# 46 instead of 36 filler products ahead of a TensorE-bound kernel, and 20 more behind the last turn of batch 0's q

## The chip, the core and the metric

The kernel runs on one core of a Trainium2 chip. The metric is the device time of one execution in microseconds (us); lower is better. The engines of the core are TensorE (PE in the profile, its weight loads PEld), VectorE (DVE), ScalarE (ACT), GpSimd (POOL) and SyncE (SP, which only starts transfers here). Each engine works through its own list of instructions in order, and waits where an instruction needs a result of another engine or of a transfer.

## The reference

Eight batches, each with 8 heads, 576 tokens and a head size of 64. Attention without softmax, each row normalised by its root mean square, then a gated linear unit with a causal convolution over 5 tokens as gate:

```python
kv = np.einsum('bhsd,bhse->bhde', k, v)
out = np.einsum('bhsd,bhde->bhse', q, kv)
rms = np.sqrt(np.mean(out * out, axis=-1, keepdims=True) + 1e-06)
attn = out / rms * g_norm                       # then (B,H,S,D) -> x of (B, S, 512)
for j in range(5):
    gate_pre += conv_w[j][None, None, :] * xp[:, j:j + S, :]   # xp: x with 4 rows of zeros ahead
gate = 1.0 / (1.0 + np.exp(-gate_pre))
y = (gate * (x @ w_val)) @ w_out                # all float32; the weights arrive as float64
```

## The kernel before

The whole program is one list of 1,235 named steps, PLAN, written out by hand. A step issues a handful of instructions, on one engine in most cases, and the order of the steps is the order of each engine's instructions. No scheduler moves anything afterwards; only the waits are put in automatically, from which tile is read and written by whom. So an engine that waits holds back all that stands behind it in its own list.

What a batch goes through: `load_q`, `load_half` bring q, k, v in; `kv_product` (L440) makes k^T v on TensorE, in two halves of the heads, into two accumulators; `turn_q_rows` (L477, batches 0 and 1 only) turns q with 24 + 8 + 4 products against an identity, `sort_q` (L484, ACT) copies the turned q out; `kv_copy` (L450, ACT) copies k^T v out; `raw_whole` (L512) multiplies q by it; `square` (L531, ACT), `sums` (L544, DVE), `powers` (L552, POOL) and `normalise` (L561, DVE) normalise the rows; `turn_x` and `keep_x` turn them; then gate, value product and output product follow. PSUM is one pool of eight banks, and every product step takes the next free one.

In front, the plan lets TensorE begin before any data are there. `start_warm n` (L430) issues n products of the identity's first 32 columns with themselves, into a bank that nobody reads:

```python
def start_warm(n):
    for _ in range(n):
        nc.tensor.matmul(warm_bank()[0:TB, 0, 0:TB], ident[:, 0:TB], ident[:, 0:TB], start=True, stop=True)
```

A float32 product shows in the trace as two records. TensorE's list in front is: 36 fillers; `turn_q_rows 0 3`, `0 2`, `0 0` (24 products, wait for q of batch 0); `kv_product 0 0` (waits for the first halves of k and v); `turn_q_rows 0 1` and `0 4` (12 products); `turn_cw` (L414, one small transpose of the convolution's weights, cw); `kv_product 0 1` (waits for the second halves of k and v); `raw_whole 0 3`, `0 4`, `0 2`, `0 0`, `0 1`; then `turn_q_rows` of batch 1.

`turn_cw` waits for cw in float32, which a chain of steps `narrow_weight cw 0 n` makes from the 64-bit input on ACT and DVE. On ACT the list is: `narrow_weight cw 0 1` and `0 2`, `warm_up` (a table load), `sort_q 0 0`, `sort_q 0 1`, `narrow_weight cw 0 3` (L372), `sort_q 0 4`, `0 3`, `kv_copy 0 0`, `0 1`, `sort_q 0 2`, then steps on the first weight block (wval) and the squares of batch 0. So cw's third step stands behind a copy of `turn_q_rows 0 1`'s result. DVE makes its last two steps of cw (L375, L389) behind that, and only behind `keep_cw` (L418 to L420) begins with wval (L380, L363, L385).

SP's list of loads is in order too: `load_q_rows 1 1` overwrites the place of batch 0's q, so it waits until `turn_q_rows 0 4` has read it, and all later loads stand behind it.

Of the kernel before, what the change touches and what calls it, by code (L numbers as in the profile page):

```python
# [18 lines left out]
PLAN = """  # L19
load_q_rows 0 1; stage_weight cw 0; load_q_rows 0 0; load_half v 0 0; load_half k 0 0; narrow_weight cw 0 5;  # L20
narrow_weight cw 0 6; narrow_weight cw 0 0; load_half v 0 1; load_half k 0 1; narrow_weight cw 0 1;
narrow_weight cw 0 2; warm_up; stage_weight wval 1; stage_weight wval 0; start_warm 36; turn_q_rows 0 3;
turn_q_rows 0 2; turn_q_rows 0 0; kv_product 0 0; turn_q_rows 0 1; sort_q 0 0; sort_q 0 1; narrow_weight cw 0 3;
narrow_weight cw 0 4; narrow_weight cw 0 7; turn_q_rows 0 4; turn_cw; keep_cw; kv_product 0 1; sort_q 0 4;
sort_q 0 3; kv_copy 0 0; kv_copy 0 1; narrow_weight wval 1 5; narrow_weight wval 1 0; sort_q 0 2; raw_whole 0 3;
load_q_rows 1 1; narrow_weight wval 1 1; narrow_weight wval 1 6; narrow_weight wval 1 2; raw_whole 0 4;
raw_whole 0 2; load_q_rows 1 0; narrow_weight wval 0 0; narrow_weight wval 0 5; square 0 3; stage_weight wval 3;
# [821 lines left out]
```

## Time and profile before

| what | before |
|---|---|
| median of 3 runs | 306.25 us (304.12 to 307.25) |
| profiled execution, first to last instruction (span) | 304.6 us |
| PE busy | 294.8 us (97%) |
| PEld busy | 232.4 us (76%) |
| DVE busy | 269.2 us (88%) |
| ACT busy | 193.7 us (64%) |
| POOL busy | 114.9 us (38%) |
| mean granted TensorE clock | 0.993 |

The span is the profiled execution's own time from its first to its last instruction; the medians are of executions without a profile and hold what lies around the span as well. The page does not show that part by itself. Busy times are of instructions, so an engine that waits is not busy. The granted clock is a share of TensorE's full clock, from events that the trace records; ahead of the first event the trace has no record of it, and the page then prints full speed.

The chain of the page goes back from the last instruction, at each step to what released it. A stage row (a stretch of time, asked for by its bounds) gives for each engine the busy time and the number of instructions in that stretch, then the granted clock, the busy share of the DMA engines and GB/s.

### The profile page before, as it was taken

To read this page: it belongs to the slowest core of one execution; us is meant where nothing else is said; L and a number is where in the kernel's file an instruction comes from. 1 tells how busy PE (TensorE), PEld (TensorE's weight loads), DVE (VectorE), ACT (ScalarE), POOL (GpSimd) and SP (SyncE) were. 2 spreads that over 40 slices of the span, in tenths; PEclk is the share of its full clock that TensorE was granted. 3 is DMA by queue.
4 is the path that set the end of the run, shared out by engine and by line. 5 is a ranking of instruction groups with operands and counts; after the bars stand their busy time and mean duration, and the time that the engine had idled before them with its cause. 6 is when DMAs were issued, how large, how long until landed. Compare 5 with 4: busy or idle time off the path is not lost.

```text
span 304.6 us, 8977 instructions
## 1 busy us (share of the span) xinstructions
PE 294.8 (97%) x3441; PEld 232.4 (76%) x3441; DVE 269.2 (88%) x474; ACT 193.7 (64%) x596; POOL 114.9 (38%) x127
## 2 busy tenths in 40 slices
PE   7899999999999999999999999999999999999993
PEld 7788778877787785777778757787878588888582
DVE  1169999999999999999999999999999999999612
ACT  1569989999768664884586547683787354535220
POOL 3027354406568217364338352345536631000000
PEclk9979999999999999999999999999999999999999
DMA  7999998088569756988689477927411621112423
GB/s 269 343 368 343 272 302 210 4 230 269 154 147 329 231 163 167 269 220 260 173 253 294 111 175 232 326 72 214 114 48 30 169 80 34 36 42 64 103 69 103
DMA packets 32074, 55.53 MB, mean 182 GB/s; under 512 B 6166, under 2 KB 14358, under 8 KB 32032
## 3 DMA queue, kind: packets, MB, share of 16 engines
q1 hardware_dynamic: 29520, 49.76, 55.7%
q0 software_dynamic: 1632, 3.17, 4.1%
q10 hardware_dynamic: 880, 2.03, 1.8%
q8 instruction: 27, 0.44, 0.6%
q14 instruction: 15, 0.12, 0.1%
HBM read 39.21 MB, written 9.44 MB: 160 GB/s over the span
## 4 chain that ended last, share of the span: by engine, by line
PE 89%; DVE 5%; DMA 2%; issue 1%; ACT 1%; DVEq 0%; ACTq 0%; SPq 0%
PE a L774 18%; PE cb L774 14%; PE va L682 13%; PE val L633 11%; PE vc L682 6%; PE kvps L440 6%; PE raw L501 5%; PE out L720 5%; PE vb L682 4%; PE qTps L477 4%; PE raw L512 2%; PE xTps L583 2%; DMA qs<-in_q_dram 2%; DVE gate L621 2%; DVE xs L667 1%
## 5 line engine op out<-in xcount | busy, mean ns | idle before, releaser
L552 POOL TENSOR_TENSOR rt<-ss,mhalf 128x8 f32<-128x8 f32 (+3 forms) x38 | 68.9, 1822 | 101.0 <-DVE ss L544 100.8
L621 DVE SCALAR_TENSOR_TENSOR gate<-xT,cwT,gate 128x576 f32<-128x576 f32 x128 | 101.8, 809 | 1.0
L571 ACT ACTIVATE x<-raw,rt 128x64 f32<-128x64 f32 x252 | 55.8, 351 | 7.2 <-POOL rt L552 4.2
L604 POOL DMA_DIRECT2D xT<-y x48 | 26.4, 557 | 25.5 <-DVE ot L784 14.0
L633 PE MATMUL val<-xT,wval 128*128 128x288 f32 x128 | 33.0, 411 | 0.0
L774 PE MATMUL a<-wsum,sums 128*128 128x256 f32 x128 | 32.4, 382 | 0.0
L628 ACT ACTIVATE gate<-gate 128x576 f32<-128x576 f32 x32 | 22.0, 692 | 11.7 <-DVE gate L621 11.4
L633 PEld LDWEIGHTS val<-xT,wval 128*128 128x128 f32 x128 | 23.5, 190 | 6.5 <-ACT xT L590 0.4
L544 DVE TENSOR_REDUCE ss<-sq 128x8 f32<-128x520 f32 (+1 forms) x40 | 24.7, 627 | 2.9 <-ACT sq L531 2.5
L774 PEld LDWEIGHTS a<-wsum,sums 128*128 128x128 f32 x128 | 24.0, 190 | 4.1 <-issue 0.6
L535 ACT ACTIVATE sq<-raw 128x256 f32<-128x256 f32 (+1 forms) x70 | 22.4, 403 | 7.3 <-PE raw L501 7.1
L682 PE MATMUL va<-xs,vsum 128*128 128x288 f32 x96 | 26.6, 409 | 0.0
L615 ACT ACTIVATE gate<-xT,cwT 128x576 f32<-128x576 f32 x32 | 25.2, 811 | 1.5 <-DVE gv L646 1.3
L646 DVE TENSOR_TENSOR gv<-gv,gate 128x576 f32<-128x576 f32 x32 | 23.6, 750 | 0.9 <-ACT gate L628 0.8
L682 PEld LDWEIGHTS va<-xs,vsum 128*128 128x128 f32 x96 | 18.0, 190 | 5.1 <-ACT x L571 0.4
L611 POOL COPY xT<-xT 128x124 f32<-128x124 f32 x32 | 17.5, 585 | 10.5 <-ACT xT L590 10.5
L501 PEld LDWEIGHTS raw<-kv,qT 64*64 64x64 f32 x1008 | 16.4, 134 | 5.3 <-issue 3.0
L440 PEld LDWEIGHTS kvps<-v,k 64*64 64x64 f32 x1008 | 15.9, 135 | 3.7 <-issue 1.9
L501 PE MATMUL raw<-kv,qT 64*64 64x64 f32 x1008 | 18.7, 221 | 0.0
L440 PE MATMUL kvps<-v,k 64*64 64x64 f32 x1008 | 17.6, 220 | 0.0
L774 PE MATMUL cb<-wsum,sums 128*128 128x256 f32 x64 | 16.9, 386 | 0.1
L774 PE MATMUL cb<-wout,gv 128*128 128x256 f32 x64 | 16.8, 385 | 0.0
(111 smaller groups left out, 542.3 us busy)
## 6 DMA issues: line engine op xcount, KB each, us to landing
qs<-in_q_dram SPq DMA_DIRECT2D x96, 140.0 KB, 4.2
out_dram<-ot SPq DMA_DIRECT2D x140, 64.0 KB, 1.7
k<-in_k_dram SPq DMA_DIRECT2D x14, 576.0 KB, 6.3
v<-in_v_dram SPq DMA_DIRECT2D x12, 576.0 KB, 6.5
xT<-y SPq DMA_DIRECT2D x48, 64.0 KB, 2.7
xT<-y POOLq DMA_DIRECT2D x48, 64.0 KB, 3.3
y<-in_moe_w_val_dram SPq DMA_DIRECT2D x4, 512.0 KB, 11.4
w_wout<-in_moe_w_out_dram SPq DMA_DIRECT2D x4, 512.0 KB, 6.3
```

What stands on the lines that cost most here:

```text
L440: nc.tensor.matmul(st["kvps", b][s][r * D:(r + 1) * D, i], st["k", b, i][rows, r, cols], st["v", b, i][rows, r, cols], start=(j == 0), sto ...
L501: nc.tensor.matmul(st["raw", b, c][r][cols, to * D:(to + 1) * D], st["qT", b][rows, hp, first:first + D], kvs[b % 2][rows, hp, :], start=T ...
L544: nc.vector.reduce_sum(out=st["ss", b][:, FIRST[c]:FIRST[c] + n], in_=st["sq", b, c][:, 0:n], axis=AX.X)
L552: nc.gpsimd.tensor_tensor(out=st["rt", b][:, which], in0=st["ss", b][:, which], in1=mhalf[:, which], op=ALU.pow)
L571: nc.scalar.activation(out=x[:, to * D:(to + 1) * D], in_=raw[:, h * D:(h + 1) * D], func=AF.Copy, scale=root[:, to:to + 1])
L604: (nc.sync if i % 2 else nc.gpsimd).dma_start(out=xTs[b % 2][i * TB:(i + 1) * TB, :, first:first + P], in_=y[a * TB:(a + 1) * TB, i])
L615: nc.scalar.activation(out=gate[:], in_=xTs[b % 2][:, jt, HALO:SX], func=AF.Copy, scale=cwT[:, K - 1, jt:jt + 1])
L621: nc.vector.scalar_tensor_tensor(out=gate[:], in0=xTs[b % 2][:, jt, tap * TB:tap * TB + S], scalar=cwT[:, tap, jt:jt + 1], in1=gate[:], op ...
L633: nc.tensor.matmul(val[:], wval[:, kc, jt * P:(jt + 1) * P], xTs[b % 2][:, kc, HALO + n * SV:HALO + (n + 1) * SV], start=(kc == 0), stop=( ...
L646: nc.vector.tensor_tensor(out=both, in0=both, in1=st["gate", b, jt][:], op=ALU.mult)
L682: nc.tensor.matmul(st[bank, "val", b, mj][:], weights_[:, k], tokens()[:, k], start=(n in (0, 1, 3) and k == 0), stop=(k == NK // 2 - 1), ...
L774: nc.tensor.matmul(st[bank, i, p], tokens()[:, k], weights_[:, k], start=(n < 2 and k == 0), stop=(k == NK // 2 - 1), skip_group_check=True)
```

## The change

`start_warm 36` becomes `start_warm 46`, and a step `start_warm 20` is put between `turn_q_rows 0 4` and `turn_cw`. Nothing else is edited.

```diff
 narrow_weight cw 0 2; warm_up; stage_weight wval 1; stage_weight wval 0;
-start_warm 36; turn_q_rows 0 3;
+start_warm 46; turn_q_rows 0 3;
 turn_q_rows 0 2; turn_q_rows 0 0; kv_product 0 0; turn_q_rows 0 1; sort_q 0 0; sort_q 0 1; narrow_weight cw 0 3;
-narrow_weight cw 0 4; narrow_weight cw 0 7; turn_q_rows 0 4; turn_cw; keep_cw; kv_product 0 1; sort_q 0 4;
+narrow_weight cw 0 4; narrow_weight cw 0 7; turn_q_rows 0 4; start_warm 20; turn_cw; keep_cw; kv_product 0 1; sort_q 0 4;
```

(The first line of the plan is broken in two here, to show its edit alone.) The fillers' bank is now in use until the second batch of them. With that, the banks of three later steps come from other tiles: `turn_cw` takes a bank that ACT has emptied where it took one that TensorE had written alone; `raw_whole 0 2` no longer has a wait on TensorE's own earlier writing, and `raw_whole 0 0` has one. The lists of DVE, ACT, POOL and SP, and all waits in them, stay as they are.

## The prediction

> **What bounds the kernel now.** I read the chain of waits first, for the first 40 us (start, length, what; both in us):
>
> ```profile
> 0.75 5.33 DMA qs<-in_q_dram
> ...
> 6.12 5.05 PE qTps L477 x48
> 11.17 1.21 PE kvps L440 x72
> 12.38 1.49 PE qTps L477 x24
> 13.86 1.19 issue
> 15.05 0.21 PE cwps L414
> ...
> 17.15 6.32 PE raw L512 x40
> 23.47 2.77 PE qTps L477 x48
> ```
>
> Two things stand out. TensorE has nothing to do for 1.19 us ahead of `turn_cw`. And equal work has unequal prices: 48 records of `turn_q_rows` cost 5.05 us at 6.12 and 2.77 at 23.47. So I asked for the groups of TensorE between 6.1 and 10.4, and between 10.6 and 13.9 (busy us, mean ns of one behind the first bar):
>
> ```profile
> L477 PE MATMUL qTps<-ident,qs 128*64 128x128 f32 x39 | 4.5, 424 | 0.7 <-DMA qs<-in_q_dram 0.7
> ...
> L477 PE MATMUL qTps<-ident,qs 128*64 128x128 f32 x35 | 2.5, 287 | 0.0
> ```
>
> The first stretch runs at about half clock, although the stage rows print 1.00 there (no record yet). Next the stages around the drop that is recorded, and a long one behind it:
>
> ```profile
> 13.93:17.34 3.41, 1.73 (x74) 1.59 (x75) 2.53 (x9) 1.86 (x7) 0.00 (x0) 1.00 0.77 253
> 17.34:20.75 3.41, 3.41 (x18) 2.65 (x18) 1.81 (x4) 3.32 (x7) 0.00 (x0) 0.50 1.01 374
> 20.75:23.47 2.72, 2.72 (x26) 2.60 (x27) 1.82 (x5) 1.72 (x4) 2.08 (x2) 1.00 1.04 396
> 22.35:107.90 85.55, 85.55 (x1369) 69.03 (x1367) 84.69 (x147) 73.41 (x225) 41.94 (x37) 1.00 0.76 227
> ```
>
> The clock was 0.50 for 3.41 us. Counted back from 17.34 in steps of 3.41, marks fall at 13.93, 10.51, 7.10 and 3.69; 10.51 is where the turns become fast. So I take it that the clock is set at such marks, by how busy TensorE was since the mark before. The records bear out: 7.10 to 10.51 busy throughout, then full; 3.69 to 7.10 with the hole between fillers and q, no rise; 13.93 to 17.34 busy for 1.73 of 3.41 us, then half.
>
> The last row says what a gain in front is worth later: from 22.35 to 107.90 PE is busy for all 85.55 us, DVE for 84.69. Both are full. The list of DVE's waits from 22.4 to 200 has three lines, 1.3 us in all, the first of them ending at that stretch's start:
>
> ```profile
> DVE ss L544 <- ACT sq L531: 0.9, 1, 0.9
> DVE x L561 <- POOL rt L552: 0.2, 1, 0.2
> DVE gv L646 <- ACT gate L628: 0.2, 1, 0.2
> ```
>
> So a gain reaches the end only as far as DVE gets it too.
>
> **The change, part by part.** *Ten more fillers.* 72 records start at 1.36; the last ends 4.05 us later and one lasts 241 ns (its group), so starts are (4.05 - 0.24) / 71 = 53.7 ns apart, 107 ns a product. 92 records let q's turns begin at 1.36 + 92 x 0.0537 = 6.30 instead of 6.12: **+0.18 us** at once. The hole between 5.41 and 6.12 is gone, the window 3.69 to 7.10 is full, and I expect full clock from 7.10. The half-clock turns cost 4.28 us for 39 records, less the start-up 0.21 us a product; at full clock (2.84 - 0.28) / 47 records give 0.109. So 24 products take 0.80 us to 7.10 (3.8 of them) and 20.2 x 0.109 = 2.20 behind it: 9.30 instead of 11.10. There the next wait is late: the first half of v is issued at 1.20 and lands 8.3 us later, 9.5. `kv_product 0 0` starts at 9.5, **1.6 us earlier**.
>
> *Down to `turn_cw`.* What follows keeps its lengths: `sort_q 0 1` came 2.35 us behind that start (13.45), now 11.85; ACT is busy with `sort_q 0 0` until 11.96, so 11.95, and the chain to `turn_cw` (13.45 to 15.05, 1.6 us) ends at 13.55, 1.5 us earlier. Next late is the second half of v: issued 1.69, landing 12.1 us later, 13.8. `kv_product 0 1` starts at about 13.9 instead of 15.19: **-1.3 us** for it, for `kv_copy` (16.56 to 15.27) and for `raw_whole 0 3` (17.15 to 15.85).
>
> *Twenty more fillers.* No row shows a filler at full clock. Upper end 107 ns a product, 2.14 us for 20; lower end half of that, 1.07, since the turns' price halved (0.21 to 0.109) and `kv_product`'s records follow each other in 1.21 / 72 = 17 ns, so issue sets no floor at 53. I take 1.07. `turn_q_rows 0 4` is issued by 12.0, the fillers end near 13.1, `turn_cw` comes at 13.55: hidden. At 2.14 they would hold `turn_cw` to 14.15 and cost 0.4. The new wait of `turn_cw` on ACT is for a copy ahead of cw's own third step in ACT's list, so it is met: 0.
>
> *The clock drop.* Without filler, the mark at 17.34 saw 51% busy. In the changed kernel 13.93 to 17.34 lacks only some 0.7 us ahead of `raw_whole`, about 80% busy: I expect no drop. `raw_whole`'s 20 products then cost 0.21 us each (half of the 17.34 to 20.75 pace, where about 8 took 3.41), 4.3 us, with 0.4 of waiting for the second `kv_copy`: from 15.85 to 20.55 instead of 23.47, **-2.9 us on TensorE**.
>
> *What ACT and DVE get of it.* ACT goes without a break from `kv_copy` to `narrow_weight wval 1 3` (20.02 to 20.73), so -1.3 there: 19.43. Then it waited 0.99 us for `raw_whole 0 2`, which is now there by 19.1: `square 0 2` at 19.43 instead of 21.72, -2.3. DVE's 0.9 us wait for that square goes; behind it `normalise 0 3` waits for POOL's power (2.06 us behind a sum that ends at 19.55): 21.7, and DVE's list reaches it at 21.8 instead of 23.95: **-2.15 us**. From there DVE has no idle time to give up. TensorE runs up to 2.9 early until it meets DVE's or ACT's results; the chain does at 89 to 108, where it goes over DVE and ACT.
>
> The loads do not spoil this. SP's queue is released by `turn_q_rows 0 4` at 12.2 instead of 13.88, and the DMA engines, at 147 GB/s between 13.86 and 15.05, fill that hole; q of batch 1 landed by 19.2 and is used from 20.55.
>
> **Sum:** +0.18 is inside the -1.3, -1.3 and the drop make -2.9 on TensorE, and DVE lets -2.15 through. The profiled span of 304.6 becomes 302.45; the median 306.25 becomes **304.1 us**. Median and span are 1.65 apart, of which I know no split; a run at 304.12 lies below the profiled span, so executions differ by more than my gain.
>
> The Trainium skill, "TensorE: Matmul & The Clock Gate", Part 1, has the clock at half until a busy window of 3.4 us and windows that run free of the kernel's start; the trace agrees on the length (3.41). It has the clock fall only after about such a window of idleness, and here 1.73 us of 3.41 were busy: the measurement decides (by that rule the second fillers save nothing, rival 2). The phase of the windows, which no single trace shows, makes both gains vary by run. By the same Part an undecoded product costs about 62 ns of sequencer time; the fillers' 53.7 ns are below that, and by 62 the twenty would take 2.5 us, the sum 0.35 less than at 2.14.
>
> **Rivals.**
> 1. *More comes through.* DVE's results may be used later than they are made, so TensorE's -2.9 reaches the end: 303.35. And the unprofiled runs may hold a second window at half clock (3.41 us, 1.7 of loss) that the fillers avoid: down to 301.65. For: the spread of 3.1 us between runs. Against: DVE without idle time. 0.25.
> 2. *One gain alone.* The drop comes anyway, or seldom came: -1.3, 304.95. For: other phases of the marks split the 1.19 us hole. Against: this trace's drop stands right behind it. 0.15.
> 3. *Small products count little as activity.* 32 of 128 columns are used. Then no mark moves: +0.18, 306.4. For: the window 3.69 to 7.10, four fifths busy, did not raise the clock. 0.10.
> 4. *Slower.* As 3, and the second fillers are paced by issue, not by the clock: 2.14 us from 13.85 end at 16.0, so `turn_cw` waits 0.95 us longer. It decides from 1.38 us for the twenty (turns issued by 13.67, cw there at 15.05), 69 ns a product. +1.15: 307.4. Against: `kv_product`'s 17 ns. 0.08.
>
> **How the numbers follow.** The forecast's chance is 0.42, its own range 303.4 to 304.9. The range 301.65 to 306.9 takes in rivals 1 to 3 and leaves out most of 4 and scatter. A measurement tells about 1% from no change: below 303.2 is faster, above 309.3 slower. Faster: most of rival 1 (0.20) and a quarter of the forecast (0.10), 0.30. Slower: a run-to-run shift on top of rival 4, 0.05. Same: the rest.
>
> **What would show it.** The turns at 287 rather than 424 ns from about 7; `turn_cw` near 13.55; the fillers of the second batch 27 ns apart; no 0.50 behind 17; `raw_whole` done near 20.6; DVE early by 2.1 us at 24. Wrong if the clock rises no earlier, if the drop comes back, or if DVE's list shows new waits later on.

## The result, and the profile after

| | before | changed |
|---|---|---|
| median of 18 runs each | 304.5 us | 307.85 us |
| lowest to highest | 304.12 to 307.25 | 305.7 to 311.72 |
| profiled execution, span | 304.6 us | 307.3 us |
| mean granted clock of it | 0.993 | 0.996 |

The changed kernel is slower by a factor of 1.0093, 95% interval 1.0067 to 1.0118; this factor leaves out the run at 311.72 us, which fell in a slower state of the chip. Forecast was 304.1 us, within 301.65 to 306.9. The profile of the changed kernel is of an execution at 309.12 us, above its median; a second one, at 307.07 us, comes below. In the profiled executions the clock is better and the time is worse.

The chain of waits of the changed kernel in front (start, length, what; us):

```profile
1.19 9.62 DMA v<-in_v_dram
10.81 0.04 issue
10.86 1.28 PE kvps L440 x72
12.13 1.46 PE qTps L477 x24
13.60 1.38 PE warm L430 x40
14.98 0.17 PE cwps L414
15.14 1.28 PE kvps L440 x72
```

The hole of 1.19 us ahead of `turn_cw` is gone, and the first turns of q are quick (timeline):

```profile
6.00 3.01 PE L477 MATMUL qTps<-ident,qs 128*64 128x128 f32 x48 [0.39 <-DMA qs<-in_q_dram]
```

These 48 records took 5.05 us in the profile of before. But the chain now begins with v's first half, 9.62 us from issue to landing where the prediction reckoned 8.3. `kv_product 0 1` starts at 15.14; before, it was 15.19. Nothing of the 1.3 us has arrived.

The stages that answer to those shown of before (busy us and count for PE, PEld, DVE, ACT, POOL; then clock, DMA share, GB/s):

```profile
13.93:17.34 3.41, 2.77 (x109) 2.50 (x105) 2.65 (x10) 1.77 (x7) 0.00 (x0) 1.00 0.86 272
17.34:20.75 3.41, 3.34 (x31) 2.92 (x30) 1.85 (x5) 3.35 (x7) 0.00 (x0) 1.00 1.03 373
...
22.35:107.90 85.55, 84.62 (x1347) 67.69 (x1344) 83.81 (x145) 72.33 (x223) 41.40 (x37) 1.00 0.76 225
```

Second row: 1.00 where it was 0.50, so the drop has gone. Last row: PE, busy for all 85.55 us before, lacks 0.93. The waits of TensorE between 17 and 295 us name where (engine, line, releaser: us in total, times, longest):

```profile
PE raw L501 <- issue: 2.1, 2, 1.4
PE kvps L440 <- DMA k<-in_k_dram: 1.2, 1, 1.2
```

In the profile of before neither line is there; its longest wait in that stretch is 0.6 us. And DVE's list from 22.4 to 200 has three new lines of about a microsecond, its first three (the one line of 0.9 us of before, for L531, is gone):

```profile
DVE ss L544 <- ACT sq L535: 1.0, 1, 1.0
DVE qT L463 <- DMA qs<-in_q_dram: 0.9, 1, 0.9
DVE ot L784 <- ACT gv L703: 0.8, 1, 0.8
DVE x L561 <- POOL rt L552: 0.2, 1, 0.2
```

"issue" means that the engine waited for nothing that the profile shows. The chain of the changed kernel at the first of these two places, in the midst of one step's products:

```profile
86.06 1.66 PE raw L501 x100
87.73 0.65 issue
88.38 0.70 PE raw L501 x25
```

and the same step in the profile of before, in one piece:

```profile
87.07 2.10 PE raw L501 x128
```

TensorE stops between two products of one step, with all their operands there. So four questions: why v lands late; why TensorE stops; whether the clock's gain is worth what was reckoned; and what the profile of before stood for.

### The profile page after: what moved, and what is told of

The parts are those of the page before. It is cut to its first block, busy times and chain, and to the rows that moved or that the text cites. A ratio compares the mean times of both kernels' runs of the same rounds, so it can differ in the third digit from the quotient of the medians.

```text
span 307.3 us, 9096 instructions
## 1 busy us (share of the span) xinstructions
PE 293.8 (96%) x3501; PEld 231.1 (75%) x3501; DVE 269.5 (88%) x474; ACT 193.7 (63%) x596; POOL 114.9 (37%) x127
## 3 DMA queue, kind: packets, MB, share of 16 engines
HBM read 39.21 MB, written 9.44 MB: 158 GB/s over the span
## 4 chain that ended last, share of the span: by engine, by line
PE 69%; DMA 13%; DVE 7%; SPq 4%; issue 2%; ACT 2%; POOL 1%; ACTq 0%; DVEq 0%
PE a L774 14%; PE va L682 11%; PE val L633 11%; PE cb L774 10%; PE kvps L440 5%; PE vc L682 5%; PE raw L501 5%; DMA out_dram<-ot 4%; PE vb L682 3%; SPq L806 3%; DMA v<-in_v_dram 3%; DMA qs<-in_q_dram 3%; DMA k<-in_k_dram 2%; PE out L720 2%; DVE gate L621 2%
## 5 line engine op out<-in xcount | busy, mean ns | idle before, releaser
L501 PEld LDWEIGHTS raw<-kv,qT 64*64 64x64 f32 x1008 | 16.9, 134 | 7.6 <-issue 5.4
L501 PE MATMUL raw<-kv,qT 64*64 64x64 f32 x1008 | 19.4, 221 | 2.1 <-issue 2.1
L463 DVE STREAM_TRANSPOSE qT<-qs 128x512 f32<-128x512 f32 x24 | 16.7, 695 | 0.9 <-DMA qs<-in_q_dram 0.9
L774 PE MATMUL cb<-wout,sums 128*128 128x256 f32 x64 | 16.7, 383 | 0.3 <-ACT ot L788 0.3
```

The source lines that it names most:

```text
L501: nc.tensor.matmul(st["raw", b, c][r][cols, to * D:(to + 1) * D], st["qT", b][rows, hp, first:first + D], kvs[b % 2][rows, hp, :], start=T ...
L774: nc.tensor.matmul(st[bank, i, p], tokens()[:, k], weights_[:, k], start=(n < 2 and k == 0), stop=(k == NK // 2 - 1), skip_group_check=True)
```

## The theory, and its rival

One queue in section 3 of the profile's page answers to the added products, first before, then changed:

```profile
q8 instruction: 27, 0.44, 0.6%
```

```profile
q8 instruction: 28, 0.46, 0.6%
```

TensorE's own instructions come during the run, 16 KB at a time (0.44 MB in 27). A float32 product is two weight loads and two products in the trace, 4 instructions; 3,441 PE and as many PEld records make 6,882, and with the semaphore instructions some 7,000, so one transfer is about 256 instructions. I counted TensorE's records (products, weight loads and semaphore instructions) from the start of the trace: every stop inside a step lies at a number of 193 plus a multiple of 256 (3009 and 3521 in the changed kernel). These numbers I call edges. Each of the twelve profiles has as many edges as transfers, 27 or 28. The transfers' times are in the trace's records of the queue.

*Block theory.* 30 more products are 120 instructions, so the edges behind them fall on other steps. That costs (a) a wait where two edges come so close together that the transfer begun at the first isn't there at the second, and (b) in front, where the loads keep all 16 DMA engines busy, a part of v or k that stands behind the 16 KB on its DMA engine. *Rival:* the number of instructions doesn't matter; fillers cost by their time, by the banks that they move, by the power that they draw, or because an earlier schedule makes later loads collide (the rival that the expectations below name).

The Trainium skill, "Runtime: NRT & Kernel Launch", section "Instruction fetch mechanics", describes these transfers: blocks of 16 KiB, 256 instructions, which an engine's sequencer fetches over a DMA queue of its own while it works on the block before. The trace agrees (16 KB, period 256). The Trainium skill calls the crossing of a boundary there "mostly hidden"; it gives TensorE room for 2,048 instructions, and a few lines further on for only two blocks. The waits below come at the very next edge, which fits two blocks and not 2,048; so here the measurement decides.

## The experiments

In the diffs `start_warm n w m` issues n fillers with w columns and m rows of weights, both 32 where not given. Only products that nobody reads are changed; all else is computed as before. Times are medians, with the kernel before on the same chip beside them.

**Each part alone (experiments 1 and 2).**

```diff
-start_warm 36; turn_q_rows 0 3;
+start_warm 46; turn_q_rows 0 3;
```

> Only the first half of the change: 46 fillers in front, none behind the last turn. Block theory: TensorE's instructions (a weight load and a product for each record, so four for each float32 product) arrive in blocks of 256 by 16 KB transfers; ten products more shift all later block edges by 40 instructions. The edge in the turns of q is reached near 6.2 us instead of 8.5, its transfer starts near 8 and holds one part of the first half of v until about 10.8, so the front gains nothing although the turns run at full clock; the clock drop at 17 remains. With 40 the edges fall outside the dense products of batch 3 and 4 (88 and 108 us), so none of the waits of 0.9 and 1.6 us seen there in the changed kernel: 304 to 305 us. Rival theory, that TensorE being earlier makes later loads collide: the same front as before, so also about 304.5, and this run does not tell them apart but prices the half. If ten fillers alone cost the 2 to 3 us, both theories fall.

Measured: 305.46 us (304.26 to 307.16) against 304.8, ratio 1.0022 (0.9997 to 1.0048).

```diff
-turn_q_rows 0 4; turn_cw;
+turn_q_rows 0 4; start_warm 20; turn_cw;
```

> Only the second half: 36 fillers in front, 20 behind the last turn. No drop to half clock at 17 us, raw_whole ends about 1.5 us earlier and DVE is about 1 us early from 24 us on, as in the changed kernel. Block theory: 80 instructions of shift put one pair of block edges 3.0 us apart at batch 3 (near 88 us), none at 108: a wait of 0 to 0.9 us there and the rest of the gain kept, 303.3 to 304.5 us. Rival theory (an earlier schedule makes later loads collide): DVE's 1 us lead is lost and more with it, 306 to 308 us, with the waits at 108 and 142 us there as well.

Measured: 305.55 us (304.83 to 308.25) against 304.8, ratio 1.0022 (0.9995 to 1.0050). Neither part alone is a gain, and neither makes the loss. Both came out above what was expected, and in the first the transfer began at 8.81 us, not near 8, so v was on time in its profile (table below). With 40 more instructions no step of TensorE stops behind 17 us; with 80, one does, near 87 us (the same list of waits as above):

```profile
PE raw L501 <- issue: 0.3, 1, 0.3
```

**Time and count apart (3 and 4).** First the fillers' time without their count: 36 products in all, some of them with 128 columns.

```diff
-start_warm 36; turn_q_rows 0 3;
+start_warm 20 128; start_warm 6; turn_q_rows 0 3;
-turn_q_rows 0 4; turn_cw;
+turn_q_rows 0 4; start_warm 10 128; turn_cw;
```

> The change's filler times with the number of fillers of before: in front 20 products of 128 columns and 6 of 32 (about 4.9 us at half clock, as 46 of 32), behind the last turn 10 of 128 columns (about 1.1 us at full clock, as 20 of 32). 36 in all, so every block edge behind turn_cw is where it was before. Block theory: no waits at 88 and 108 us, the first fetch starts later than 9.5 us, so v lands near 9.5 and turn_cw comes near 13.6 us: the gain that was forecast for the change comes through, 302 to 303 us. Rival theory (the earlier schedule makes later loads collide): as slow as the changed kernel or slower, 306.5 to 309 us, since the schedule is earlier still.

Measured: 306.9 us (306.5 to 307.12) against 304.8, ratio 1.0064 (1.0040 to 1.0089). A miss: the wide products cost twice what I had reckoned, and `turn_cw` came at 16.39 us (chain of waits):

```profile
14.09 2.30 PE warm L430 x20
16.39 0.17 PE cwps L414
```

It still tells two things. TensorE has no "issue" wait of 0.3 us or more behind 17 us. And the 2.9 us by which `turn_cw` is later than in the good run of before (13.49, below) arrive almost whole at the end: the span is 305.1 against 302.3. Lateness in front isn't absorbed.

Then the count alone: 66 small products in front (16 columns, 16 rows), as many instructions as in the changed kernel, none in the gap.

```diff
-start_warm 36; turn_q_rows 0 3;
+start_warm 66 16 16; turn_q_rows 0 3;
```

> The change's number of fillers (66) in about the time of before's: 66 products of 16 x 16 columns in front, none behind the last turn. Gap and clock drop as before, so TensorE's and DVE's schedule up to 80 us is that of before within 0.5 us. Block theory: the block edges behind turn_cw are those of the changed kernel (120 instructions of shift), so the waits near 88 us (about 0.9) and 108 us (about 1.6) come, 306 to 308 us. Rival theory (the earlier schedule makes later loads collide): nothing is earlier, 304 to 305 us.

Measured: 307.38 us (306.6 to 310.93) against 304.8, ratio 1.0101 (1.0036 to 1.0166): the whole loss. The same step stops, at records 3009 and 3521 again (waits of TensorE, 17 to 295 us), while the gap ahead of `turn_cw` is open as before, 1.2 us:

```profile
PE raw L501 <- issue: 1.4, 2, 0.9
```

v's last part lands at 10.57 us. (The clock of this profile rose late, at 9.26 us, so not all of its late front is v's.) So the loss goes with the count, and neither with the fillers' size nor with their place in the gap; nor with the banks, which are those of before here, since there is no second batch.

**The kernel before, once more (5).**

> The kernel before, unchanged, once more, for a second trace of it. Its 20 times in the last comparison fall in two groups, 304.0 to 304.9 and 305.4 to 306.5. If the trace of before that the prediction used (span 304.6, a clock drop at 17 us) belongs to the upper group, then a run in the lower one has a span near 302.5, TensorE at full clock by about 7 us, and no drop at 17 us: DVE some 2 us earlier from 24 us on. Then what the fillers can win is won already in most runs of before. If a run near 304.2 shows the drop as well, the two groups have another cause.

Measured: 304.1 us, span 302.3. This execution differs from the profile that the prediction was made from (chain of waits in front):

```profile
1.20 8.20 DMA v<-in_v_dram
...
9.44 1.28 PE kvps L440 x72
10.72 1.49 PE qTps L477 x24
12.21 1.28 issue
13.49 0.21 PE cwps L414
...
13.71 1.35 PE kvps L440 x72
```

The hole in front of `turn_cw` is as long (1.28), but all of it is 1.5 us earlier, since the clock was full from 4.73 us on (the trace's clock record) and not from 10.51; nor did it drop later. So the unchanged kernel has most of the forecast's front by itself: `kv_product 0 0` at 9.44 (forecast 9.5), `kv_product 0 1` at 13.71 (forecast 13.9). By the mean clock of 55 runs of before: 32 at 0.995 or more have a median of 304.28 us (303.98 to 305.86), 23 below it 306.24 (304.86 to 308.43). The groups overlap. The profile with 0.993 was of the second kind.

**Count right, size right (6).** As the third, with fewer wide products:

```diff
-start_warm 36; turn_q_rows 0 3;
+start_warm 6 128; start_warm 20; turn_q_rows 0 3;
-turn_q_rows 0 4; turn_cw;
+turn_q_rows 0 4; start_warm 4 128; start_warm 6; turn_cw;
```

> As e3_same_count, with the sizes set by what that run measured (a product of 128 columns cost 0.43 us at half and 0.22 at full clock, one of 32 columns 0.107 and 0.065): in front 6 of 128 and 20 of 32 columns, about 4.7 us at half clock; behind the last turn 4 of 128 and 6 of 32, about 1.3 us at full clock. 36 in all, so all block edges behind turn_cw are where before has them. Block theory: no waits at 88 and 108 us, v on time (9.4), no drop at 17 us in nearly all runs: 303.8 to 304.6 us with few runs above 305, as fast as the lower group of before and 1% below the changed kernel. Rival theory (an earlier schedule makes later loads collide): 306 to 308 us.

Measured: 304.22 us (304.05 to 305.28) against 304.95, ratio 0.997 (0.9938 to 1.0003). The edges are those of before, the waits at 88 and 108 are absent, and all twelve runs have a clock of 0.995 or more. This is what the fillers are good for: the 306 us group doesn't occur. The interval still takes in no change at all. (One wait of 0.4 us, at 34.9, is an edge too: record 1217.)

**A whole block more (7).** If only the place of the edges counts, 256 instructions more than before (64 products) must give back the old places behind the front:

```diff
-start_warm 36; turn_q_rows 0 3;
+start_warm 80 16 16; turn_q_rows 0 3;
-turn_q_rows 0 4; turn_cw;
+turn_q_rows 0 4; start_warm 20; turn_cw;
```

> The changed kernel with 34 fillers more: 80 of 16 x 16 columns in front (about 4.3 us at half clock, against 4.9 for 46 of 32), 20 of 32 columns behind the last turn. 64 products more than before are 256 instructions, one whole block, so the edges behind turn_cw fall where before has them. Block theory: the first edge comes inside the fillers, its transfer before 8.7 us, v lands near 10.7 as in the changed kernel; but the waits at 88 and 108 us go, and with them 2 to 3 us: 304.8 to 306 us, faster than the changed kernel (307.85) with more fillers. Rival theory (fillers cost by their number, or the earlier schedule collides): 307.5 us or more.

Measured: 307.67 us (306.77 to 309.04) against 304.95, ratio 1.0066 (1.0028 to 1.0104). For the waits the theory holds: "PE raw L501 <- issue" is gone from the list behind 17 us. The time is a miss, because an edge in front, record 705, now falls into `kv_product 0 1`, which the expectation had left out (chain of waits):

```profile
14.97 0.26 PE kvps L440 x4
15.23 1.31 issue
16.54 1.22 PE kvps L440 x63
```

With that wait the half clock is back, behind a stretch in which PE was busy for 1.61 of 3.41 us (stages):

```profile
14.88:18.29 3.41, 1.61 (x73) 1.32 (x72) 3.18 (x9) 0.50 (x2) 0.00 (x0) 1.00 0.98 343
18.29:21.70 3.41, 3.34 (x17) 2.73 (x17) 0.34 (x2) 3.32 (x8) 0.00 (x0) 0.50 1.02 358
```

Against the good run of before, DVE is 3.6 us late at 24 us and 3.4 at the end: all of the loss is in front, and nothing is lost behind it.

**Ten in the gap (8).**

```diff
-turn_q_rows 0 4; turn_cw;
+turn_q_rows 0 4; start_warm 10; turn_cw;
```

> 36 fillers in front, 10 behind the last turn: the shift of 40 instructions of e1_front_only, whose profiled run had no TensorE wait at 88 or 108 us, with half the filler in the gap. Block theory: no waits there; fillers of 0.7 us leave 0.5 to 0.8 us of idle time in the gap, so the drop at 17 us comes seldom: 304.0 to 304.9 us, fewer runs above 305.4 than before has. Rival theory (earlier schedule collides): as e2_gap_only or slower, 305.5 us and more.

Measured: 304.46 us (304.0 to 306.03) against 304.95, ratio 0.9968 (0.9936 to 0.9999). With 40 instructions more no step stops at 88 or 108. With the sixth, this is the best of all; both are about 1% below the changed kernel. Both have a second batch of fillers, and so the banks of the changed kernel, and a front as early as in the good run of before, without the loss. With the fourth, this leaves neither the banks nor the earlier schedule as the cause. The third has more filler time and none of these stops, the fourth has the stops without it. No run varies the power alone; in both profiles of the changed kernel the clock stays full from its rise to the last 3 us.

**The count behind the front (9).** 30 small products in the gap, so that the first edge and v's landing stay as they were and only the later edges move:

```diff
-turn_q_rows 0 4; turn_cw;
+turn_q_rows 0 4; start_warm 30 16 16; turn_cw;
```

> 36 fillers of 32 columns in front as before, 30 of 16 x 16 columns behind the last turn: the number of the changed kernel (66) with before's front. Block theory: the first edge and its transfer are where before has them, so v is on time (9.4); the edges behind turn_cw are the changed kernel's, so TensorE waits near 86 us (about 0.8) and near 106 us (about 1.1 to 1.6) although e8_gap_ten, with 20 fillers fewer at the same place, has neither: 306 to 308 us. If the loss of the changed kernel came from its longer front alone, this run is as fast as e8_gap_ten plus what 30 small products outlast the gap, 304.5 to 305.2 us.

Its four runs scatter from 305.99 to 311.79 us, median 309.57 against 304.28, ratio 1.0183 (1.0102 to 1.0264); two of them have a mean clock of 0.984 and 0.987, and what they did isn't known. The others are 305.99 and 308.12 us, so this ratio is no price. The profiled one is the fastest, 305.99 us, clock 0.996.

```profile
PE raw L501 <- issue: 1.6, 2, 1.4
```

That is its list of waits behind 17 us. v is on time (`kv_product 0 0` at 9.48), and TensorE stops at 86.79 and 107.62. A third edge, record 705, hides behind another wait (5 to 17 us):

```profile
PE raw L512 <- ACT kvbd L450: 1.2, 1, 1.2
```

With 66 fillers `raw_whole` begins at this record, and the profile puts the whole wait down to `kv_copy`. But here `raw_whole` starts 0.61 us behind the end of the second `kv_copy` (at 16.39 us, 1.40 behind a transfer's landing), where ten of the twelve profiles have 0.05 or 0.06. Against the good run of before, DVE's instructions are 0.14 us early at 15 us, 0.20 late from 19, 0.63 late from 88 and 1.50 late from 110 on. So the two waits behind 17 us, with v on time, cost 1.3 us, and the one in front 0.3.

**The changed kernel, once more (10).**

> The changed kernel once more, for a second trace. Block theory: the waits of TensorE inside the 64 x 64 products near 87 and 107 us are there again, at the same instructions (number 193 of a block of 256), of some 0.5 to 1.7 us each; the last part of v lands after 10.5 us if the first transfer of instructions begins before 8.7, else near 9.4. 305.7 to 309.5 us. If the waits stand at other instructions or are gone while the time is still 2 us above before's, the block theory does not explain the loss.

Measured: 307.07 us, span 305.2, clock 1.000. The chain in front, and TensorE's waits behind 17 us:

```profile
9.37 1.28 PE kvps L440 x72
10.65 0.80 PE qTps L477 x11
11.45 0.54 issue
11.99 0.98 PE qTps L477 x13
```

```profile
PE raw L501 <- issue: 2.0, 2, 1.1
```

The two waits come back at the same records (87.92 and 108.49 us). But v is on time (9.37), and in its place TensorE stops among the turns, at record 449, and at record 705 (`raw_whole` starts 0.37 us behind `kv_copy`, at 16.67).

**What an edge needs.** From the trace's records of transfers and products: the stops between two products of one step in four profiles, and for comparison the edges at the same steps in the good run of before (us; "goes on" is where TensorE passes the next edge, the last column the difference of the two ahead of it):

| kernel | edge before | transfer lands | TensorE goes on | behind the landing |
|---|---|---|---|---|
| changed | 84.43 | 86.88 | 88.38 | 1.50 |
| changed | 105.65 | 107.71 | 109.21 | 1.50 |
| changed, again | 6.26 | 10.54 | 11.99 | 1.45 |
| changed, again | 83.80 | 86.56 | 87.92 | 1.36 |
| changed, again | 105.19 | 107.08 | 108.49 | 1.41 |
| 30 small in the gap | 83.26 | 85.30 | 86.79 | 1.49 |
| 30 small in the gap | 104.06 | 106.10 | 107.62 | 1.52 |
| a whole block more | 10.88 | 15.15 | 16.54 | 1.39 |
| before (no stop) | 85.14 | 86.87 | 93.03 | 6.16 |
| before (no stop) | 104.19 | 106.28 | 115.20 | 8.92 |

TensorE goes on 1.36 to 1.52 us after the landing at each stop; at those of the second, fourth and sixth experiment it is 1.32 to 1.56. In the rows behind 80 us the transfers begin 0.7 to 1.2 us behind an edge and take 1.0 to 1.7, and TensorE, where it stopped, went on 3.3 to 4.1 us behind the edge before. One step of `raw` is 128 PE records and 128 weight loads, as many instructions as a whole block, in 2.10 us. Where such a step is cut decides, and 120 instructions cut it elsewhere.

All twelve profiles bear out the landing: with edges and transfers both taken in order, no edge is passed sooner than 1.16 us behind the landing of the transfer that belongs to the edge before. The start is less regular. Of 329 transfers 251 begin behind their edge, by up to 10.3 us, and 78 ahead of where I count it, by up to 4.5 us. So edges more than 4 us apart aren't safe either: the stop at 34.89 us in the sixth experiment is 7.6 us behind the edge before, because the transfer began only 4.9 us behind that.

In front the same transfer is slower to begin (2.0 us behind the edge in the changed kernel, 3.2 in its other run), and when it begins decides what it hits. Start of the first transfer, and landing of the 15th and the last of the 16 parts of v's first half:

| kernel | transfer starts | 15th part | last part |
|---|---|---|---|
| 66 small | 6.88 | 9.30 | 10.57 |
| a whole block more | 7.07 | 9.31 | 10.60 |
| changed | 8.24 | 9.37 | 10.81 |
| front alone | 8.81 | 9.36 | 9.36 |
| changed, again | 9.50 | 9.33 | 9.33 |
| before, good run | 10.27 | 9.37 | 9.40 |

Up to 8.24 the transfer holds one part back by 1.3 to 1.4 us; from 8.81 on it leaves v's first half alone. The second half bears this out. In the eleven profiles whose first transfer starts by 11.06 us its last part lands at 13.46 to 13.80 us, and the other 15 by 12.45; in the third experiment, whose transfer starts at 13.27, all 16 are there by 12.42. That the transfer holds the part back on a DMA engine that both use is inferred from these times; the trace doesn't name the engines.

## Why the prediction was wrong, point by point

*What bounds the kernel: right.* PE and DVE are full, and what is lost in front is still lost at the end (third and seventh experiment).

*The base: wrong.* I took the profile's 304.6 us span as the kernel's usual execution. It was one of the group whose clock comes late and drops again, and 306.25 us was the median of three runs; of 18 it is 304.5. The other group, 304.28 us median, has most of the forecast's front already, as its profile shows (fifth experiment). I had seen that a run at 304.12 lay below the profiled span, and wrote it off as scatter; it was the answer to what the gain could be. In the sixth experiment the fillers remove the 306 us group and gain nothing beyond that (304.22).

*Half clock until 7.10: wrong in size, harmless.* The clock was full from 4.21 and 5.04 us in the two profiles of the changed kernel. TensorE's groups of the changed kernel up to 17 us, all fillers and all turns of batch 0 (busy us, mean ns of one, idle ahead of it):

```profile
L430 PE MATMUL warm<-ident 128*32 128x32 f32 x132 | 5.7, 214 | 1.4 <-POOL ident masks.py:199 1.4
L477 PE MATMUL qTps<-ident,qs 128*64 128x128 f32 x72 | 4.5, 275 | 0.4 <-DMA qs<-in_q_dram 0.4
```

*`kv_product 0 0` at 9.5: the step that failed first.* In the profile it is 10.86, in the other one 9.37. "The loads do not spoil this" looked at SP's loads, and not at the queue that brings TensorE's own instructions.

*Twenty fillers 1.07 us, hidden: mis-sized.* Their 40 records start 32 ns apart, 65 ns a product where I took 53, 1.38 us in the chain. By the measured chain to cw they delay `turn_cw` by 0.1 us at most.

*No drop at 17.34: right*, but the reason given isn't the whole of it. The only other drop seen, in the seventh experiment, again follows a stretch half empty (1.61 of 3.41 us, against 1.73 before). Yet in the first profile of the changed kernel PE was busy for only 1.57 us from 7.62 to 11.04, a stretch counted in steps of 3.41 from its rise at 4.21, and no drop came. So the busy share alone doesn't decide, and what does is open. *`raw_whole` done at 20.55:* 21.95 (16.99 and 4.96 us), since it began 1.1 us later than forecast.

*DVE lets 2.15 us through, and has no idle time later on: the step that decided.* DVE was 1.0 us early against the profile of before from 24 to 89 us. Then the two stops of TensorE, and late loads, take that and more: 0.1 early behind 90, 0.75 late behind 113, 1.9 behind 148 (loads that land late) and 2.8 at the end. Its three new waits stand at these places: at 89.79 us for squares that follow the first stop, at 113.40 for a copy behind the second, and at 149.76 for a part of q. The prediction moved the steps and held their lengths; it did not see that a step's length depends on where the instruction list is cut. The prediction named new waits on DVE's list as what would make it wrong; they came.

*The rivals.* The time came nearest to the fourth (307.4), but by another mechanism: the clock does rise and the fillers aren't slow enough to matter. No rival had the instructions' own transfers.

*The sum.* Against the good run of before (span 302.3), the changed kernel's DVE is later by 1.37 us from v on, 0.85 more at 88, 0.86 at 110, 1.15 by 149 (most of it at 149.76, its wait for q), 0.73 at 217: 4.96, of a span 5.0 longer. Its other profile: 0.74 in front (v on time, but the stops at records 449 and 705), 1.02 at 88, 0.60 at 110 and 0.5 later make 2.9, of a span 2.9 longer. The two stops are in both, 1.6 to 1.7 us, and the lowest times of the two kernels are 1.58 apart. What is above that varies by run: which load the first transfer hits in front, and loads that land late, q for DVE (above) and k for TensorE:

```profile
135.12 7.23 DMA k<-in_k_dram
142.35 0.14 issue
142.48 1.28 PE kvps L440 x72
```

A 16 KB transfer runs from 138.96 to 139.91 there; that it holds parts of these loads back is likely by the front's pattern, but not shown. Open as well: why a transfer begins now ahead of its counted edge (2.2 us at 113 us in the eighth experiment) and now up to 10 us behind it (some records can be missing from the traces, so the count can drift); and the 0.7 us at 217, which the kernel with 20 in the gap shows too (1.1 us there), without the changed kernel's front.

## What to carry to other kernels

Instructions that do no work aren't free, even where their time is hidden: they shift every later cut between two blocks of that engine's instructions, and a step of small dense products that was cut at the wrong place stopped here for 0.2 to 1.4 us. So count instructions as well as time: prefer a few wide fillers to many narrow ones (36 products with some wide ones did what 66 didn't), look in the trace for "issue" waits inside one step, look first where two cuts are within some 4 us of each other, and mistrust a wait that is longer than the step that it is put down to explains (`raw_whole` behind `kv_copy`). And before reckoning a gain from one profile, see which group of the kernel's runs that profile belongs to; a gain that the better runs already have is no gain.

## What the runs showed of the hardware that was not expected

- TensorE's instructions arrive in 16 KB transfers during the run, one for every 256 records. At the stops TensorE goes on 1.3 to 1.6 us behind such a transfer's landing, and in twelve profiles it passes no edge sooner than 1.16 us behind it.
- One such transfer, about 1 us long, goes, by the times of the table above, with a delay of 1.3 to 1.4 us for one of 16 parts of a load in front, where the DMA engines are full (DMA share 1.02 to 1.07 from 3.69 to 13.93 us of the changed kernel), and a consumer waits for the last part.
- The start of full clock varies between executions of one kernel: 4.73 and 10.51 us for the kernel before.
- The clock dropped to 0.50 behind stretches of 3.41 us with PE busy for 1.73 and 1.61 us, and not behind one with 1.57.
- A float32 filler of 32 columns and 32 rows takes 65 ns at full clock, against 107 ahead of the clock's rise: more than half of it. One of 16 columns and 16 rows hardly changes: its records start 27 ns apart ahead of the rise (fourth experiment) and 25 ns behind it (ninth).
- A 128-column float32 product takes 0.23 us at full clock (ten, 20 records, in 2.30 us).
